# Moving the operands of the main products to other places within 512 bytes, in a windowed attention with a rational feed-forward layer

## The chip, the cores and the metric

The kernel runs on one core of one Trainium2 chip. The metric is the device time of one execution in microseconds; three runs of the kernel before gave 959.98 (median), 959.06 and 960.10 us. A profile of one further execution is read here as "the profile"; the engines in it are PE (TensorE, matrix products), PEld (the loads of stationary operands for them), DVE (VectorE), ACT (ScalarE), POOL (GpSimd) and SP (the queue that issues the transfers).

## What is computed

The reference is a causal attention with a window of 64 positions (8 batches, 8 heads, 576 positions, 64 channels), whose output becomes 4608 tokens of 512 channels, followed by a two-layer feed-forward part with a rational function between the layers:

```python
scores = where(mask, q @ k.T / sqrt(64), -1e9)      # 0 <= i - j < 64
x = (softmax(scores) @ v).transpose(0, 2, 1, 3).reshape(4608, 512)
h = x @ w_in                                         # 512 -> 2048
P = a[0] + a[1]*h + a[2]*h**2 + a[3]*h**3
Q = 1 + abs(b[0])*abs(h) + abs(b[1])*h**2
out = (P / (Q + 1e-6)) @ w_out                       # 2048 -> 512
```

## The kernel before

The tokens are taken in 12 chunks of 384 (`CH`), the 2048 inner channels in 16 blocks of 128. One pair of a chunk and a block is a **step**; there are 192. A step has three parts.

*First layer* (`ffn1`, lines 597 to 607). PE multiplies a 128 x 128 block of `w_in` with the chunk's `x`, 384 tokens wide, for each of the four groups of 128 input channels. To reach fp32 accuracy every operand is kept as two parts, a high one and a low one (`xh`, `xl`, `wi_h`, `wi_l`), and three products are added: `wi_h` with `xl`, `wi_h` with `xh`, `wi_l` with `xh`. That is 4 x 3 = 12 products for a step, each with the weight block as the **stationary** operand (loaded into the array ahead of the product, a PEld row) and 384 columns of `x` as the **moving** operand (streamed through the array, a PE row). All are written to a PSUM tile `h`.

*Gate* (`gate`, lines 609 to 628). ACT and DVE work out the rational function from `h` and leave the result as two parts `gh` and `gl`. Except for four steps at either end this is done for two steps at once, on tiles with two halves of 384 columns.

*Second layer* (`ffn2`, lines 638 to 668). For each of three groups of 128 tokens, PE multiplies 128 columns of `gl` or `gh` (stationary now) with a block of `w_out` (`wo_h`, `wo_l`: moving, 512 columns): 3 x 3 = 9 products for a step, added up over the 16 blocks in three PSUM tiles `o0` to `o2`.

So each core has 192 x 12 = 2304 products of 384 columns and 192 x 9 = 1728 products of 512 columns. While one product streams, the stationary operand of the next one is being loaded: both are read from the same on-chip memory (SBUF), at two addresses in the same partition.

The attention units (12 chunks x 4 pairs of heads) are strewn between the steps: `ps_s<-qk` (scores), the exponentials on ACT, `ps_s<-ident,sm` (transposes on PE) and `ps_x<-sm,vt` (values). They leave the next chunk's `xh` and `xl` in one of two slots (`x_slot`, line 456). The weights are in two halves as well: blocks 0 to 7 in the tiles `wi_h0`, `wi_l0`, `wo_h0`, `wo_l0` of the pool `const`, blocks 8 to 15 in tiles of the pool `late`. All operations are recorded first, by a planner (lines 55 to 277) that gives each a cost and a start, and are issued in the order of those starts; so nearly every row of the profile has line 277.

**Where things lie.** A pool hands out its tiles one behind the other in every partition, each rounded up to 32 bytes, and the three pools `const`, `late` and `ring` follow each other. `shift` (line 377) makes a tile that nothing uses, to move what comes behind it. Adding up the declarations gives each operand's **place**, its address modulo 512. Blocks of `w_in` (512 bytes), of `w_out` (2048), the `x` tiles (1536), the halves of a gate tile (1536) and a gate tile (3072) are all whole multiples of 512 bytes, so that in the kernel before every operand of a kind has one place:

- `const` opens at byte 1152; ident, ident_b, mask, ab_sb, b_sb and warm take 512 + 256 + 1536 + 32 + 32 + 256; the weights begin at 3776, place 192.
- Four weight tiles of 16384, two `top` tiles of 2048 and the shift of 80 words (320 bytes) later, `x` begins at 73728, place 0.
- Sixteen `x` tiles and the shift of 48 words later `late` begins at 98496, place 192 again.
- `ring`, from 164032, has qk (3360), two vt (3072 each), three w_st (4128 each), two sm (3072 each), six small ones (32 each), six tmp (3072 each) and the shift of 32 words; the gate tiles begin at 210816, place 384.

The **distance** of a product is here the place of its stationary operand less that of its moving operand, modulo 512. Before, it is 192 - 0 = 192 in the first layer and 384 - 192 = 192 in the second, six units of 32 bytes in both.

Of the kernel before, what the change touches and what calls it, by code (L numbers as in the profile page):

```python
# [10 lines left out]
F32R = mybir.dt.float32r  # L11
# [10 lines left out]
CH = 384  # L22
# [4 lines left out]
PAIRS = 2, 2  # L27
# [9 lines left out]
JOIN = 4  # L37
LOADS = "q0 q1 w0 v0 q2 v1 q3 w1 v2 v3 w2 w3 w4 w5 w6 w7 w8"
WLEAD = 4
NEG = -8.0e9  # L40
QADD = 1.0 + 1e-6


class Late:


    def __init__(self, key, start, size, get):
        self.key, self.start, self.size, self.get = key, start, size, get
# [239 lines left out]
class Slots:  # L288


    def __init__(self, pool, n, shape, dtype, name):
        self.tiles = [pool.tile([shape[0], 2, *shape[1:]], dtype, name=f"{name}_{k}") for k in range(n)]
        self.n = 0

    def __call__(self, size):
# [16 lines left out]
def swa_rational_ffn(ctx: ExitStack, tc: tile.TileContext, qk, v, w_in, w_out, out):  # L312
    nc = tc.nc
    P = 128
    HP = qk.shape[0]
# [8 lines left out]
    const = ctx.enter_context(tc.tile_pool(name="const", bufs=1))  # L324
    late = ctx.enter_context(tc.tile_pool(name="late", bufs=1))
    ring = ctx.enter_context(tc.tile_pool(name="ring", bufs=1))
# [16 lines left out]
    def make_mask():  # L343
# [3 lines left out]
        def block(j, h, empty):  # L347
            r = mask[half[h], j, :]
            nc.gpsimd.memset(r, 0.0)

            nc.gpsimd.affine_select(out=r, in_=r, pattern=[[1, P]], compare_op=ALU.is_ge, fill=NEG,
                                    base=-WIN if empty else -1, channel_multiplier=0 if empty else -1)

            nc.gpsimd.affine_select(out=r, in_=r, pattern=[[-1, P]], compare_op=ALU.is_ge, fill=NEG, base=WIN, channel_multiplier=1)

# [21 lines left out]
    def shift(pool, words, name):  # L377
        pool.tile([P, words], F32, name=name)

    H = NF // 2  # L380
    W_SHAPES = dict(wi_h=[P, H, NCC, P], wi_l=[P, H, NCC, P], wo_h=[P, H, DO], wo_l=[P, H, DO])
    w_sb = {(n, 0): const.tile(shape, F32R, name=f"{n}0") for n, shape in W_SHAPES.items()}

    def late_tile(name):
        if (name, 1) not in w_sb:
            w_sb[name, 1] = late.tile(W_SHAPES[name], F32R, name=f"{name}1", tag=f"late_{name}")
        return w_sb[name, 1]

    def weight(name, i, view=lambda x: x):
        if i < H:  # L390
            return view(w_sb[name, 0][:, i])
        return Late(f"late_{name}", (i - H) * 2048, 2048, lambda: view(late_tile(name)[:, i - H]))

    def weight_piece(name, i, cc):
        if i < H:
            return w_sb[name, 0][:, i, cc, :]
        return Late(f"late_{name}", (i - H) * 2048 + cc * 512, 512, lambda: late_tile(name)[:, i - H, cc, :])

# [1 line left out]
    for t in tops:  # L400
        nc.vector.memset(t, 0)

    shift(const, 80, "before_x")
    x_sb = [[[const.tile([P, CH], F32R, name=f"x{part}{s}{hp}") for hp in range(HP)] for part in "hl"] for s in range(2)]
    shift(const, 48, "after_x")
    early = [late.tile([P, H * DO], F32, name=f"early{k}", tag=f"late_{n}") for k, n in enumerate(("wo_l", "wo_h"))]
    QK = 2 * CH + WIN
    QKAB = QK + 6
# [9 lines left out]
    sm_ring = Ring(ring, 2, [P, 2, PR, P], F32, "sm")  # L418
    small = {n: Ring(ring, 2, [P, 2 * PR], F32, n) for n in ("nmx", "sums", "rs")}
    tmp = Slots(ring, TMP, [P, CH], F32, "tmp")  # L420
    shift(ring, 32, "before_g")
    g_ring = [Slots(ring, n, [P, CH], F32R, name) for n, name in zip(PAIRS, ("gh", "gl"))]
    ob_ring = Ring(ring, 2, [P, DO], F32, "ob")

    shares = {t.tensor.name: f"late_{n}" for t, n in zip(early + spare, ("wo_l", "wo_h", "wi_h", "wi_l"))}
# [207 lines left out]
    part = {}  # L633
# [38 lines left out]
    def at(s, *call):  # L672
        todo.setdefault(max(s, 0), []).append(call)

    for i in range(H):
        if i >= WLEAD:
            at(i - WLEAD, load_weight, "in", i)
        at(i, load_weight, "out", i)
    second = [("in", i) for i in range(H, H + WLEAD)]
    for i in range(H, NF):  # L680
        if i + WLEAD < NF:
            second.append(("in", i + WLEAD))
        second.append(("out", i))
    for n, key in enumerate(second):
        at(H - 1 + n, load_weight, *key)
    fetch_order += [("in", i) for i in range(WLEAD)]
    fetch_order += [tuple(call[1:]) for s in range(total) for call in todo.get(s, ()) if call[0] is load_weight]

    s, seen, places = 0, {0}, []
# [21 lines left out]
    for load in LOADS.split():  # L711
        what, k = load[0], int(load[1])
# [71 lines left out]
```

## Time and profile before

| | |
|---|---|
| median of three runs | 959.98 us (959.06 to 960.10) |
| the profiled execution's own time | 959.31 us |
| its span, first to last instruction | 957.5 us |
| PE busy, share of the span | 947.7 us, 99% |
| DVE busy | 853.2 us, 89% |
| ACT busy | 666.2 us, 70% |
| products of 384 columns (`h<-...`) | 3 x 768 |
| products of 512 columns (`o<-...`) | 3 x 576 |

Busy time on PE counts each product from its dispatch to its modelled end, so successive products overlap: a row's mean duration (336 ns for 384 columns) is not what a product costs. What it costs is the distance in time from its start to the next one's start, the **spacing**, which is read from the timeline or from the chain of waits, where runs of products are merged with their count.

### The profile page before, as it was taken

What the parts mean: (1) busy time and instruction counts of PE and PEld (TensorE: products, weight loads), DVE (VectorE), ACT (ScalarE), POOL (GpSimd) and SP (SyncE); (2) the same over time, 40 slices, a digit from 0 to 9 for tenths busy, and PEclk for the clock granted to TensorE, in tenths of its full rate; (3) what the DMA queues carried; (4) which work ended last, traced back from release to release, by engine and by line L of the source; (5) the groups of instructions that cost most, each with busy time, mean ns of one, the idle gap of its engine ahead of it and who ended that gap; (6) DMA issues with size and microseconds to landing.
All of it is one profiled execution on the core that took longest, in us unless ns stands there. A gap on an engine that the chain in (4) does not pass through costs nothing.

```text
span 957.5 us, 17342 instructions
## 1 busy us (share of the span) xinstructions
PE 947.7 (99%) x6923; PEld 837.9 (88%) x6923; DVE 853.2 (89%) x1287; ACT 666.2 (70%) x1553; POOL 4.4 (0%) x20
## 2 busy tenths in 40 slices
PE   8999999999999999999999999999999999999998
PEld 6888888898888888888888888888888888888997
DVE  6999998899988899889988998899889988997887
ACT  7988777676676677667667667667666766665654
POOL 1000000000000000000000000000000000000000
PEclk9999999999999999999999999999999999999999
DMA  9454342131101102113112112110210311300000
GB/s 352 135 187 150 104 158 94 58 123 59 47 35 68 53 23 98 35 35 103 35 35 79 60 35 69 42 63 24 80 39 32 102 36 36 102 1 1 34 1 33
DMA packets 24560, 68.36 MB, mean 71 GB/s; under 512 B 2720, under 2 KB 2720, under 8 KB 24480
## 3 DMA queue, kind: packets, MB, share of 16 engines
q1 hardware_dynamic: 24480, 67.27, 20.5%
q8 instruction: 54, 0.88, 0.4%
q14 instruction: 26, 0.21, 0.1%
HBM read 57.03 MB, written 10.22 MB: 70 GB/s over the span
## 4 chain that ended last, share of the span: by engine, by line
PE 84%; DVE 9%; ACT 3%; DMA 2%; issue 1%; POOL 0%; SPq 0%; POOLq 0%; ACTq 0%; DVEq 0%
PE o L277 38%; PE h L277 36%; PE ps_s L277 6%; DVE tmp L277 4%; PE ps_x L277 4%; DVE gh L277 1%; DVE w_st L277 1%; ACT sm L277 1%; DVE gl L277 1%; DMA qk<-qk 1%; DVE wo_l L277 1%; ACT tmp L277 1%; DMA w_st<-w_out 1%; DVE nmx L277 1%; DVE wi_l L277 0%
## 5 line engine op out<-in xcount | busy, mean ns | idle before, releaser
L277 PE MATMUL h<-xl,wi_h 128*128 128x384 f32 x768 | 259.1, 337 | 0.1
L277 PE MATMUL h<-xh,wi_h 128*128 128x384 f32 x768 | 258.1, 336 | 0.0
L277 PE MATMUL h<-xh,wi_l 128*128 128x384 f32 x768 | 257.9, 336 | 0.0
L277 ACT ACTIVATE tmp<-h 128x384 f32<-128x384 f32 x192 | 95.1, 496 | 218.9 <-PE h L277 217.5
L277 PE MATMUL o<-wo_h,gl 128*128 128x512 f32 x576 | 236.1, 410 | 0.8 <-DVE gl L277 0.8
L277 PE MATMUL o<-wo_l,gh 128*128 128x512 f32 x576 | 228.0, 396 | 0.0
L277 PE MATMUL o<-wo_h,gh 128*128 128x512 f32 x576 | 227.7, 395 | 0.0
L277 ACT ACTIVATE tmp<-h,ab_sb 128x384 f32<-128x384 f32 x384 | 221.0, 629 | 0.0
L277 ACT ACTIVATE tmp<-tmp 128x768 f32<-128x768 f32 (+1 forms) x200 | 164.8, 824 | 16.0 <-DVE tmp L277 12.9
L277 PEld LDWEIGHTS h<-xl,wi_h 128*128 128x128 f32 x768 | 144.3, 188 | 8.4 <-DVE tmp L277 0.6
L277 PEld LDWEIGHTS h<-xh,wi_h 128*128 128x128 f32 x768 | 144.3, 188 | 6.8
L277 PEld LDWEIGHTS h<-xh,wi_l 128*128 128x128 f32 x768 | 144.4, 188 | 0.0
L277 DVE SCALAR_TENSOR_TENSOR gh<-tmp,ab_sb,tmp 128x768 fp32r<-128x768 f32 (+1 forms) x100 | 98.5, 985 | 47.8 <-ACT tmp L277 47.5
L277 PEld LDWEIGHTS o<-wo_h,gh 128*128 128x128 f32 x576 | 108.7, 189 | 25.1
L277 PEld LDWEIGHTS o<-wo_h,gl 128*128 128x128 f32 x576 | 108.5, 188 | 24.3 <-issue 6.5
L277 PEld LDWEIGHTS o<-wo_l,gh 128*128 128x128 f32 x576 | 108.7, 189 | 15.9
L277 DVE SCALAR_TENSOR_TENSOR tmp<-tmp,ab_sb,h 128x384 f32<-128x384 f32 x192 | 117.3, 611 | 2.9
L277 DVE SCALAR_TENSOR_TENSOR tmp<-tmp,b_sb,tmp 128x768 f32<-128x768 f32 (+1 forms) x96 | 96.0, 1000 | 25.8 <-ACT tmp L277 25.8
L277 DVE TENSOR_TENSOR tmp<-tmp,h 128x384 f32<-128x384 f32 x192 | 105.2, 549 | 4.4 <-ACT tmp L277 4.4
L277 DVE SCALAR_TENSOR_TENSOR tmp<-tmp,ab_sb,tmp 128x768 f32<-128x768 f32 (+1 forms) x96 | 95.9, 999 | 1.7
L277 DVE SCALAR_TENSOR_TENSOR tmp<-tmp,gh 128x768 f32<-128x768 f32 (+1 forms) x100 | 92.4, 924 | 1.4
L277 ACT ACTIVATE sm<-sm,nmx 128x128 f32<-128x128 f32 x216 | 83.6, 390 | 12.9 <-DVE nmx L277 12.9
(97 smaller groups left out, 817.2 us busy)
## 6 DMA issues: line engine op xcount, KB each, us to landing
qk<-qk SPq DMA_DIRECT2D x42, 419.0 KB, 3.2
vt<-v SPq DMA_DIRECT2D x44, 384.0 KB, 4.0
out<-ob SPq DMA_DIRECT2D x33, 256.0 KB, 2.1
w_st<-w_out SPq DMA_DIRECT2D x15, 512.0 KB, 4.3
w_st<-w_in SPq DMA_DIRECT2D x11, 512.0 KB, 3.3
early<-qk SPq DMA_DIRECT2D x6, 419.0 KB, 8.5
early<-v SPq DMA_DIRECT2D x4, 384.0 KB, 8.8
early_wi_l<-w_in SPq DMA_DIRECT2D x3, 512.0 KB, 10.0
```

The source lines that it names most:

```text
L277: call(*[value(x) for x in args], **{k: value(x) for k, x in kw.items()})
```

## The change

Only places are changed. No operation is added, removed or put in another order.

- A shift of 8 words (32 bytes) ahead of the weights moves their first half from place 192 to 224.
- The shift ahead of `x` is 72 words in place of 80, so `x` stays at 73728, place 0. Behind the eight tiles of each slot there are 16 words (64 bytes): slot 0 stays at place 0, slot 1 comes to place 64.
- The shift ahead of `late` is 88 words (352 bytes): `late`, with the second half of the weights, begins at 98784, place 480.
- The halves of a gate tile are 64 bytes further apart (`G_APART`), a tile takes 3200 bytes, and 64 words are put behind the two tiles of each part. With a shift of 56 words ahead, `gh` begins at 211200, place 256, and `gl` at 217856, place 256. The four halves of each part lie at the places 256, 320, 384 and 448.
- What lies in `ring` moves along: qk from place 192 to 480, vt from 480 to 256, sm from 64 to 352, tmp from 256 to 32.

The first layer's distances are 224 - 0, 224 - 64, 480 - 0 and 480 - 64: 7, 5, 15 and 13 units of 32 bytes. The second layer's are the four gate places less 224 or 480: 1, 3, 5, 7, 9, 11, 13 and 15 units. Together that makes twelve cases, all odd: four with 576 products each and eight with 216 each.

```diff
+X_APART = 16
+G_APART = 16
...
-    def __init__(self, pool, n, shape, dtype, name):
-        self.tiles = [pool.tile([shape[0], 2, *shape[1:]], dtype, name=f"{name}_{k}") for k in range(n)]
+    def __init__(self, pool, n, shape, dtype, name, apart=0):
+        self.tiles = [pool.tile([shape[0], 2, shape[1] + apart], dtype, name=f"{name}_{k}")[:, :, 0:shape[1]] for k in range(n)]
...
+    shift(const, 8, "before_w")
...
-    shift(const, 80, "before_x")
-    x_sb = [[[const.tile([P, CH], F32R, name=f"x{part}{s}{hp}") for hp in range(HP)] for part in "hl"] for s in range(2)]
-    shift(const, 48, "after_x")
+    shift(const, 72, "before_x")
+    x_sb = []
+    for s in range(2):
+        x_sb.append([[const.tile([P, CH], F32R, name=f"x{part}{s}{hp}") for hp in range(HP)] for part in "hl"])
+        shift(const, X_APART, f"after_x{s}")
+    shift(const, 56 + 64 - 2 * X_APART, "before_late")
...
-    shift(ring, 32, "before_g")
-    g_ring = [Slots(ring, n, [P, CH], F32R, name) for n, name in zip(PAIRS, ("gh", "gl"))]
+    shift(ring, 56, "before_g")
+    g_ring = []
+    for n, name in zip(PAIRS, ("gh", "gl")):
+        g_ring.append(Slots(ring, n, [P, CH], F32R, name, G_APART))
+        shift(ring, 64, f"after_{name}")
```

## The prediction

> **What bounds the kernel now.** First the page's shares and its chain of waits, then the chain in order of time between 860 and 950 us, where no attention work is left.
>
> ```profile
> PE 947.7 (99%) x6923; PEld 837.9 (88%) x6923; DVE 853.2 (89%) x1287; ACT 666.2 (70%) x1553; POOL 4.4 (0%) x20
> PEclk9999999999999999999999999999999999999999
> PE 84%; DVE 9%; ACT 3%; DMA 2%; issue 1%; POOL 0%; SPq 0%; POOLq 0%; ACTq 0%; DVEq 0%
> 876.02 4.16 PE h L277 x24
> 880.18 4.20 PE o L277 x18
> 884.38 4.16 PE h L277 x24
> ```
>
> PE is never idle and its granted clock is full all the time, so the chain runs through PE. The last three rows give the price of one product: 24 first-layer products take 4.16 us, 173.3 ns each; 18 of the second layer 4.20 us, 233.3 ns each. The waits and the groups say who waits for whom, and how many products there are:
>
> ```profile
> ACT tmp L277 <- PE h L277: 217.5, 149, 3.4
> PE o L277 <- DVE gl L277: 0.8, 2, 0.6
> ...
> L277 PE MATMUL h<-xl,wi_h 128*128 128x384 f32 x768 | 259.1, 337 | 0.1
> L277 PE MATMUL h<-xh,wi_h 128*128 128x384 f32 x768 | 258.1, 336 | 0.0
> L277 PE MATMUL h<-xh,wi_l 128*128 128x384 f32 x768 | 257.9, 336 | 0.0
> L277 PE MATMUL o<-wo_h,gl 128*128 128x512 f32 x576 | 236.1, 410 | 0.8 <-DVE gl L277 0.8
> L277 PE MATMUL o<-wo_l,gh 128*128 128x512 f32 x576 | 228.0, 396 | 0.0
> L277 PE MATMUL o<-wo_h,gh 128*128 128x512 f32 x576 | 227.7, 395 | 0.0
> ```
>
> ACT waits for PE for 217.5 us; PE waits for the gate's result twice, 0.8 us in all. So 3 x 768 x 173.3 ns = 399 us and 3 x 576 x 233.3 ns = 403 us, 802 of the 957.5 us, are spacing of products, and a nanosecond on each of the 4032 is 4.0 us of time. The change can only act through that spacing, or by slowing an engine that feeds PE.
>
> **Is there anything in the spacing that places could change?** The group of bf16 products has the same 384 columns, and two of them stand merged at 33.72 us:
>
> ```profile
> L277 PE MATMUL ps_s<-mask,ident_b 128*128 128x384 bf16 x20 | 5.0, 330 | 0.9 <-ACT sm L277 0.7
> 33.72 0.49 PE L277 MATMUL ps_s<-mask,ident_b 128*128 128x384 bf16 x2
> ```
>
> The pair lasts 0.49 us, one of them 0.33, so the second starts 0.16 us after the first. A product of the first layer pays 173.3 ns for as many columns, 13 ns more. The same excess at 512 columns is 233.3 - 0.16 x 512/384 = 20 ns. In all 2304 x 13 + 1728 x 20 = 65 us. It may belong to the 4-byte data itself or to the meeting of two readers, for the next stationary operand is fetched during the product:
>
> ```profile
> 501.73 0.19 PEld L277 LDWEIGHTS h<-xh,wi_l 128*128 128x128 f32 x1
> ...
> 501.73 0.33 PE L277 MATMUL h<-xh,wi_h 128*128 128x384 f32 x1
> 501.90 0.33 PE L277 MATMUL h<-xh,wi_l 128*128 128x384 f32 x1
> 502.07 0.33 PE L277 MATMUL h<-xl,wi_h 128*128 128x384 f32 x1
> 502.24 0.34 PE L277 MATMUL h<-xh,wi_h 128*128 128x384 f32 x1
> ```
>
> The load and the product start together. And here three products take 0.51 us, 170 ns each, in place of 173.3. The second layer has such a stretch as well:
>
> ```profile
> 505.73 0.39 PE L277 MATMUL o<-wo_l,gh 128*128 128x512 f32 x1
> ...
> 507.56 0.34 PE L277 MATMUL h<-xl,wi_h 128*128 128x384 f32 x1
> ...
> 509.65 0.40 PE L277 MATMUL o<-wo_h,gl 128*128 128x512 f32 x1
> ...
> 511.74 0.34 PE L277 MATMUL h<-xl,wi_h 128*128 128x384 f32 x1
> ```
>
> From 505.73 to 507.56 are eight products, 228.8 ns each; from 509.65 to 511.74 nine, 232.2 each, the last one at a turn to the other layer. Shapes and distance are equal, and only the stretch before (attention products in the first case) differs. So the spacing depends on how the two streams stand to each other in time, which is what one expects of readers that get into each other's way, and a difference of 4.5 ns (233.3 - 228.8) or 3.3 ns (173.3 - 170) is within reach of it. That is my ground for taking places seriously.
>
> **The parts of the change.**
>
> *Places of the two operands.* The trace has one distance, six units of 32 bytes, for nearly all products, and no odd one. Bounds for an odd one from the nearest rows: on the side of gain the faster stretches, 3.3 and 4.5 ns a product, and at the far end the whole excess, 13 and 20 ns. On the side of loss I take a wait of one 64-byte line of the moving stream. That is 16 columns, and 128 columns cost 233.3 - 173.3 = 60 ns, so 7.5 ns, an estimate. Nothing says that all twelve cases fall alike. I take half of them at one such wait (2016 products x 7.5 ns = 15.1 us), a quarter unchanged, and a quarter at the faster spacing (576 x 3.3 + 432 x 4.5 ns = 3.8 us). [...] Sum: +11.3 us.
>
> *Gate halves 64 bytes further apart.* DVE's pair operations on `gh` and `gl` now skip 64 bytes between two runs of 384. The trace has one operation on one stretch of 768 and on two runs of 384 in separate banks:
>
> ```profile
> L277 DVE TENSOR_REDUCE nmx<-sm 128x6 f32<-128x768 f32 x36 | 34.2, 951 | 0.0
> L277 DVE TENSOR_REDUCE nmx<-ps_s 128x6 f32<-128x768 f32 x10 | 9.6, 955 | 0.8 <-PE ps_s L277 0.8
> L277 DVE TENSOR_TENSOR gl<-tmp,tmp 128x768 fp32r<-128x768 f32 x92 | 87.9, 955 | 1.1
> ```
>
> 4 ns at most; three such operations for each of the 92 pairs make 1.1 us on DVE, beside PE. If that cover went, 1.1 us would be the cost. I take nothing.
>
> *Other tiles moved along in `ring`* (qk, vt, sm, tmp). The first chunk's units have their q, k and v in other tiles, part of them at places that are no multiples of 64 (a unit there is 6424 bytes), and their rows read:
>
> ```profile
> L277 PE MATMUL ps_s<-qk 64*64 64x128 f32 x1008 | 37.2, 278 | 0.4 <-DMA qk<-qk 0.4
> L277 PE MATMUL ps_s<-early 64*64 64x128 f32 x96 | 3.5, 278 | 0.6 <-DMA early<-qk 0.6
> L277 PE MATMUL ps_x<-sm,vt 128*64 128x64 f32 x1056 | 40.4, 226 | 0.0
> L277 PE MATMUL ps_x<-sm,early 128*64 128x64 f32 x48 | 1.9, 226 | 0.0
> ```
>
> 278 and 226 ns in both: nothing. For ACT and DVE on `tmp` no row shows an odd place. One per cent either way on DVE would be 8.5 us of its 853.2, behind a PE that waits for it 0.8 us; I take nothing, and if all that reached PE it would be 8.5 us.
>
> *Waits, queues, transfers.* None is added or moved: dependences, costs and sizes as the planner sees them are the same, so the order is.
>
> Sum: 959.3 (the profiled execution's own time, 0.7 below the median) + 11.3 = 970.6 us. About 0.2%, 2 us, is what a measurement of this kernel can tell from no change.
>
> **The rivals.**
>
> *Places do not matter (959.3 us).* For it: the turns between the layers have other distances. During the last second-layer product of a step the first layer's weights are loaded, 192 - 192 = 0 units; during the last first-layer product a gate tile, 384 - 0 = 12 units.
>
> ```profile
> 501.32 0.39 PE L277 MATMUL o<-wo_h,gh 128*128 128x512 f32 x1
> ...
> 509.47 0.34 PE L277 MATMUL h<-xh,wi_l 128*128 128x384 f32 x1
> ...
> 509.88 0.40 PE L277 MATMUL o<-wo_l,gh 128*128 128x512 f32 x1
> ```
>
> From 501.32 to 501.73 and from 509.47 to 509.88 one product of each layer passes, 0.41 us both times, where steady spacings give 0.407. So distances 0 and 12 cost what 6 costs, within 0.01 us. All three are whole lines of 64 bytes, and the change is the first to leave these: against it stands also that two stretches at one distance differ by 4.5 ns. This rival is also the Trainium skill's view: "TensorE: Matmul & The Clock Gate", section "What happens when you issue a matmul", says that PE reads its streaming operand and its weight loads through two independent SBUF ports, and that the load takes no read bandwidth from the running product. By that rule the sum is zero; the faster stretches at equal shapes speak against it, the turns for it.
>
> *Half a line apart is better (943.9 us).* If the steady spacings hold a wait that comes from both readers standing at the same point of a 64-byte line, an offset of half a line removes it, and all products run at the faster rows: 2304 x 3.3 + 1728 x 4.5 = 15.4 us. It decides as soon as odd distances agree among themselves, so that no mixture is left. At 943.9 us DVE's 853.2 would be 90%, still not the bound. The far end, the whole 65 us, would give 894 us, with DVE at 95%; no stretch of the trace comes near.
>
> *Every odd distance costs one line (989.5 us).* The same mechanism with the other sign: an operand half a line off touches nine lines in each load (first layer) or one more in each stream (second layer), and the extra one is waited for: 4032 x 7.5 = 30.2 us. It is the slow end of my forecast rather than a case of its own.
>
> **How the numbers follow.** The forecast's case, slower by a mixture or by all twelve, 0.48; no difference 0.22; half a line is better 0.30. These are also the chances of slower, same and faster. The range goes from the faster rival, 944, to all twelve at one wait, 990; beyond lie a gain nearer the whole excess and a loss of more than a line. The likeliest case alone goes from 961.3 to 990.
>
> **What the profile after would show.** In the chain, runs of `PE h` and `PE o` between 860 and 950 us: right, if 24 and 18 products no longer take 4.16 and 4.20 us and the steps differ in a rhythm of four (gate places), by weight half and by slot of `x`; then the twelve cases can be read one by one. If all steps are equal among themselves at another spacing, it is the offset of half a line, in either direction, and the mixture is wrong. If the runs stay at 4.16 and 4.20 us, places do not matter. DVE's pair rows should stay within 4 ns of 955, and PE's waits for `gl` near 0.8 us; if those grow, DVE is the cause and not the spacing.

## The result, and the profile after

The changed kernel took 965.83 us (median of four runs, 965.05 to 966.18) against 959.89 us (959.06 to 960.10): a ratio of 1.006, with a 95% interval of 1.0048 to 1.0073. It is 5.9 us slower. The profiled execution took 965.05 us, its span is 963.3 us.

First the page, with the chain's shares, and then the waits. A line of the code now has number 279 instead of 277.

```profile
span 963.3 us, 17342 instructions
PE 954.6 (99%) x6923; PEld 843.0 (88%) x6923; DVE 853.4 (89%) x1287; ACT 665.6 (69%) x1553; POOL 4.3 (0%) x20
PEclk9999999999999999999999999999999999999999
PE 92%; DVE 3%; ACT 3%; DMA 1%; issue 1%; POOL 0%; POOLq 0%; ACTq 0%
```

```profile
ACT tmp L279 <- PE h L279: 226.6, 153, 3.5
PE o L279 <- DVE gl L279: 0.9, 2, 0.7
```

The number of instructions is the same, the clock is full, DVE and ACT are as busy as they were (853.4 for 853.2, 665.6 for 666.2 us). Only PE is busier, 954.6 us for 947.7, and ACT waits longer for it, 226.6 us for 217.5. So nothing that feeds PE is in the way; PE itself takes longer over the same work. Where, the chain in order of time shows, in the stretch without attention (start in us, duration, what):

```profile
885.30 4.20 PE o L279 x18
889.50 4.23 PE h L279 x24
893.74 4.21 PE o L279 x18
897.95 4.24 PE h L279 x24
902.19 4.19 PE o L279 x18
```

24 first-layer products take 4.23 to 4.24 us, for 4.16 before: 176.5 ns each in place of 173.3. 18 of the second layer take 4.19 to 4.21 us, for 4.20.

That holds for the whole span. Adding up the time from the start of each product to the start of the next one, where both are of the same layer, gives 370.3 us before and 375.9 after for the first layer (2128 intervals, 174.0 and 176.6 ns), and 359.7 and 360.7 us for the second (1512 intervals). All other intervals together changed by -0.9 us. So the first layer alone makes 5.6 us, as much as the span grew by (5.7), and the rest cancels. The order of the instructions on PE is the same, product by product, in both traces.

The twelve cases can be read apart, since each step's weights, slot and gate half are known. Each case must be held against the same steps of the kernel before, where all have distance 6. This table is worked out from the starts in the two traces. It has the mean spacing of products with a neighbour of the same layer on both sides, in ns:

| layer | distance, units of 32 bytes | the same steps before, at 6 | after |
|---|---|---|---|
| first | 5, 7, 13, 15 | 173.2, 174.0, 173.2, 173.2 | 176.5, 175.5, 176.3, 175.7 |
| second | 1, 3, 5, 7 | 233.2, 232.9, 230.0, 233.3 | 232.4, 233.6, 233.1, 233.5 |
| second | 9, 11, 13, 15 | 233.4, 232.9, 230.3, 232.8 | 232.2, 233.9, 232.9, 233.5 |

All four cases of the first layer lost, 1.5 to 3.3 ns. Cases whose distances differ by 8 units, 256 bytes, agree within 0.2 ns there.

In the second layer a gate place is also a position among four successive steps, and the attention units come back every four steps as well. So its columns differ already before, where the distance is one: the third step of every four, whose second layer stands right behind an attention unit's score products, has 230.0 and 230.3 ns. Against the same steps the second layer lost 3.1 and 2.6 ns in these (distances 5 and 13), and the other six lie between 1.2 ns below and 1.0 above. Another kernel with all distances at 6 ("Everything half a line off", below) differs from these groups by up to 1.3 ns, so no price can be read from those six.

The rows beside PE, which the prediction had put at nothing:

```profile
L279 DVE TENSOR_TENSOR gl<-tmp,tmp 128x768 fp32r<-128x768 f32 x92 | 87.8, 954 | 1.1
L279 PE MATMUL ps_s<-qk 64*64 64x128 f32 x1008 | 37.2, 278 | 0.0
L279 PE MATMUL ps_x<-sm,vt 128*64 128x64 f32 x1056 | 40.4, 226 | 0.0
```

954 ns for 955, 278 for 278, 226 for 226: neither the gap in the gate tiles nor the tiles moved along cost anything.

### The profile page after: what moved, and what is told of

Same layout as the page of the kernel before. It is cut to its first block, busy times and chain, and to the rows that moved or that the text cites. A ratio compares the mean times of both kernels' runs of the same rounds, so it can differ in the third digit from the quotient of the medians.

```text
span 963.3 us, 17342 instructions
## 1 busy us (share of the span) xinstructions
PE 954.6 (99%) x6923; PEld 843.0 (88%) x6923; DVE 853.4 (89%) x1287; ACT 665.6 (69%) x1553; POOL 4.3 (0%) x20
## 4 chain that ended last, share of the span: by engine, by line
PE 92%; DVE 3%; ACT 3%; DMA 1%; issue 1%; POOL 0%; POOLq 0%; ACTq 0%
PE o L279 42%; PE h L279 40%; PE ps_s L279 6%; PE ps_x L279 4%; DVE tmp L279 1%; ACT tmp L279 1%; ACT sm L279 1%; DMA w_st<-w_out 1%; DVE nmx L279 0%; ACT top L279 0%; DVE gh L279 0%; DVE gl L279 0%; DVE wi_l L279 0%; DVE sm L279 0%; DVE w_st L279 0%
## 5 line engine op out<-in xcount | busy, mean ns | idle before, releaser
L279 ACT ACTIVATE tmp<-h 128x384 f32<-128x384 f32 x192 | 95.1, 495 | 226.9 <-PE h L279 226.6
```

Of the source, the lines that this page charges most:

```text
L279: call(*[value(x) for x in args], **{k: value(x) for k, x in kw.items()})
```

## The experiments

Four explanations stood at the start. A: the first layer's stationary operand is off a line of 64 bytes. B: the distance is an odd number of 32-byte units. C: the many places keep PE from one rhythm. And the rival that places do not matter, which would need another cause for the 5.9 us. All kernels below differ from the kernel before, or from the changed one where it is said, only in the lines shown; every ratio is to the kernel before. A "line of 64 bytes" is here only a stretch that begins at a multiple of 64; no run shows that the chip reads in such stretches.

### Weights alone half a line off

```diff
+    shift(const, 8, "before_w")
...
-    shift(const, 80, "before_x")
+    shift(const, 72, "before_x")
...
-    shift(const, 48, "after_x")
+    shift(const, 56, "after_x")
...
+    shift(ring, 120, "before_qk")
```

> Weights alone 32 bytes off (place 224 in both halves), x at 0, gate tiles at 384, the tiles of ring at their old places: one odd distance in each layer, 7 in the first and 5 in the second. Theory A (the first layer's stationary operand off lines of 64 bytes costs its products 2 to 3 ns, whatever the distance): 24 first-layer products take about 4.23 us instead of 4.16, the time is about 966 us. Theory B (an odd distance costs it): the same, 966. Theory C (it is the variety of places, which keeps the streams from settling into one rhythm): steady at 4.16, 960 us.

Measured: 964.65 us, ratio 1.0056 (1.0044 to 1.0069). Without the two slots, without the four gate places, with one odd distance in each layer, nearly the whole loss is there. C falls. But the loss lies elsewhere in part: added up as above, the intervals of the first layer grew by 3.2 us and those of the second by 2.8, for 5.6 and 1.0 in the changed kernel. The chain in order of time, early and late:

```profile
183.00 2.12 PE h L277 x12
191.85 4.24 PE h L277 x24
...
209.82 4.17 PE h L277 x24
...
248.50 2.08 PE h L277 x12
...
889.41 4.17 PE h L277 x24
893.58 4.19 PE o L277 x18
```

At 183 us a step's 12 products take 2.12 us, 176.7 ns each, and at 192 us 24 take 4.24, as in the changed kernel. Others take 4.17 or 2.08, nearly as before, and in the undisturbed stretch all take 4.17 from 881 us on. So an odd distance is not always slow: at this one, 7, slow and fast steps alternate where attention units stand between them, and all are fast where none do.

### The other operands half a line off

The same odd distances from the other side: x and gate tiles moved, the weights left.

```diff
-    shift(const, 80, "before_x")
+    shift(const, 88, "before_x")
...
-    shift(const, 48, "after_x")
+    shift(const, 40, "after_x")
...
-    shift(ring, 32, "before_g")
+    shift(ring, 40, "before_g")
```

> x and the gate tiles 32 bytes off instead of the weights (x at 32, gate at 416, weights at 192): distances 5 and 7, odd; now the moving operand of the first layer and the stationary one of the second are off lines of 64. Theory A, carried over to the second layer: the first layer stays at 4.16 us for 24, the second's 18 products take some 2 to 3 ns more each, 4.24 us instead of 4.20, time about 964 us; A for the first layer alone: 960. Theory B: the first layer slow as in the changed kernel, 966 us. Theory C: 960 us.

Measured: 966.00 us, ratio 1.0062 (1.0048 to 1.0076).

```profile
890.60 4.23 PE h L277 x24
894.83 4.19 PE o L277 x18
```

The first layer is slow at 4.23 us, although its stationary operand is on a line of 64 again. Its intervals grew by 6.7 us, those of the second layer by 0.1. A falls, in both forms: the second layer, whose stationary operand is off a line now, stays at 4.19.

### Everything half a line off

```diff
+    shift(const, 8, "before_w")
...
+    shift(ring, 120, "before_qk")
...
-    shift(ring, 32, "before_g")
+    shift(ring, 40, "before_g")
```

> Weights, x and gate tiles all 32 bytes off lines of 64 (224, 32, 416): both distances are 6 again, even, as before. Theory A: the first layer is slow, since its stationary operand is off a line: 966 us or more. Theory B: both distances are even, so all is as before, 960 us. Theory C: 960 us.

Measured: 959.53 us, ratio 0.9998 (0.9989 to 1.0006).

```profile
182.95 2.08 PE h L277 x12
191.71 4.16 PE h L277 x24
...
892.55 4.16 PE h L277 x24
896.71 4.20 PE o L277 x18
```

All three kinds of operand lie 32 bytes off lines of 64, and every spacing is as before. So for this move of 32 bytes it is the distance between two operands that counts, not the place of any one of them. This also answers the rival: places matter through distances.

### The changed kernel with even distances

```diff
-    shift(const, 8, "before_w")
...
-    shift(const, 72, "before_x")
+    shift(const, 80, "before_x")
...
-    shift(const, 56 + 64 - 2 * X_APART, "before_late")
+    shift(const, 48 + 64 - 2 * X_APART, "before_late")
...
-    shift(ring, 56, "before_g")
+    shift(ring, 64, "before_g")
```

(against the changed kernel)

> The changed kernel with its weights back on lines of 64 (places 192 and 448): gate parts at four places, weights at two, x at two, and twelve even distances (4, 6, 12, 14 in the first layer, 0 to 14 in the second). Theories A and B: 960 us, both layers at their old spacing if even distances are alike. Theory C (variety): 966 us. If single distances differ, the steps differ by gate place, weight half or x slot, and a distance better than 6 would show here.

Measured: 960.46 us, ratio 1.0007 (0.9998 to 1.0015). The variety is the same as in the changed kernel, the loss is gone. But even distances are not alike, and the time is a balance: the first layer's intervals grew by 2.4 us, those of the second shrank by 1.8. Worked out as in the table above, in ns:

| layer | distance | the same steps before, at 6 | spacing |
|---|---|---|---|
| first | 4, 12 | 173.2, 173.2 | 175.7, 175.7 |
| first | 6, 14 | 174.0, 173.2 | 173.3, 173.3 |
| second | 2, 10 | 233.2, 233.4 | 233.4, 233.3 |
| second | 4, 12 | 232.9, 232.9 | 232.5, 232.6 |
| second | 6, 14 | 230.0, 230.3 | 230.0, 230.3 |
| second | 0, 8 | 232.8, 233.3 | 228.8, 228.8 |

So B in its plain form falls as well: 4 and 12 are even, and cost the first layer 2.5 ns, about what the odd ones cost. The first layer's price repeats after 256 bytes. In the second layer distances 0 and 8 are better than 6, by 4.0 and 4.5 ns; the others differ from the same steps before by 0.4 ns at most.

### Distance 0 in the second layer

```diff
-    shift(ring, 32, "before_g")
+    shift(ring, 112, "before_g")
```

> The kernel before with its gate tiles at place 192 in place of 384, like the weights: distance 0 in the second layer, 6 in the first. In the run with twelve even distances the second layer's steps at distances 0 and 8 had 228.3 ns a product against 233.3 at the steady distance 6. Theory D (each distance modulo 256 bytes has a rhythm of its own, and 0 is better than 6): 18 products take 4.11 us or less instead of 4.20, first layer 4.16 as before; 1728 x 5 ns = 8.6 us, about 951 to 952 us. Theory E (those steps were fast because of what came before them in that mixture): 4.20 us, 960 us.

Measured: 954.57 us, ratio 0.9948 (0.9936 to 0.9961): the fastest kernel of this study, ahead of the kernel before by 5 us and of the changed one by 11.

```profile
888.81 4.16 PE h L277 x24
892.97 4.09 PE o L277 x18
897.06 4.16 PE h L277 x24
```

Theory D holds, with less than it forecast. In the undisturbed stretch 18 products take 4.09 us in place of 4.20, 227.2 ns each. Over the span the second layer's intervals shrink by 4.9 us, not by 8.6. The forecast took 228.3 against 233.3 ns on all 1728 products, but the span's means are 228.9 and 232.3, over 1512 intervals. The third step of every four, at 230.0 and 230.3 ns before, gained next to nothing (230.2 and 229.9).

### Two other distances in the first layer

Each in addition to the edit above; x at place 192, then at 128.

```diff
-    shift(const, 80, "before_x")
+    shift(const, 128, "before_x")
...
-    shift(const, 48, "after_x")
```

> As the run with distance 0 in the second layer, and x at place 192 too: distance 0 in both layers. If what is good for 512 columns is good for 384, the first layer gains as well: 2304 x 3 to 5 ns = 7 to 12 us more, about 940 to 945 us. If a multiple of four units is bad for the first layer (distances 4 and 12 cost it 2.3 ns a product in the mixture of even distances): about 957 us.

```diff
-    shift(const, 80, "before_x")
+    shift(const, 112, "before_x")
...
-    shift(const, 48, "after_x")
+    shift(const, 16, "after_x")
```

> As the run with distance 0 in the second layer, and x at place 128: distance 2 in the first layer, the last even one not yet seen there. If parity is all: first layer as before, 4.16 us for 24, about 952 us. If each distance has its own spacing: another value, between 4.08 and 4.24 us for 24, 948 to 956 us.

Measured: 961.75 us, ratio 1.0022 (1.0013 to 1.0030), for distance 0; 959.95 us, ratio 1.0000 (0.9991 to 1.0009), for distance 2. Both lie above all that was expected of them. The chain of the first and then of the second:

```profile
887.49 4.18 PE h L277 x24
891.68 4.12 PE o L277 x18
```

```profile
885.66 4.24 PE h L277 x24
889.90 4.08 PE o L277 x18
```

Distance 0, good for 512 columns, costs the first layer 0.02 us for 24 even where it is undisturbed (175.7 ns over the span, worked out as in the tables), and distance 2, though even, 0.08. The second layer has distance 0 in these two kernels and in the one before them, and takes 4.12, 4.08 and 4.09 us, although only x was moved: it depends on the first layer's operands as well.

### 16 bytes

All x tiles become slices of one tile, which begins 16 bytes ahead of them; nothing else moves.

```diff
-    x_sb = [[[const.tile([P, CH], F32R, name=f"x{part}{s}{hp}") for hp in range(HP)] for part in "hl"] for s in range(2)]
-    shift(const, 48, "after_x")
+    x_all = const.tile([P, 4 + 4 * HP * CH + 4], F32R, name="x_all")
+    x_at = lambda n: x_all[:, 4 + n * CH:4 + (n + 1) * CH]
+    x_sb = [[[x_at((2 * s + part) * HP + hp) for hp in range(HP)] for part in range(2)] for s in range(2)]
+    shift(const, 40, "after_x")
```

> The kernel before with x 16 bytes off (all sixteen x tiles in one tile, place 16): distance 176 bytes, 5.5 units, in the first layer; nothing else moves. If the two streams meet in lines of 64 bytes, and only the share of a line counts, the first layer lies between distance 6 (4.16 us for 24) and 5 (4.23): about 963 us. If a grain of 32 bytes counts and 16 stay within it: 960 us. If the grain is 16 bytes: any value, with its own rhythm.

Measured: 958.61 us, ratio 0.9987 (0.9978 to 0.9996).

```profile
884.37 4.20 PE h L277 x24
888.58 4.14 PE o L277 x18
```

The first layer is half way between 4.16 and 4.23, as the first reading expected, but the time isn't. What none expected: the second layer, none of whose operands moved, takes 4.14 us in place of 4.20, and the kernel comes out 1 us faster. Over the span the first layer's intervals grew by 1.8 us and those of the second shrank by 3.4. So a layer's spacing depends on the other layer's operands too.

### Does the stream meet the next load, or its own operand?

In both kernels xl and wi_l alone are 32 bytes off; the second also changes the order of each three products.

```diff
-    w_sb = {(n, 0): const.tile(shape, F32R, name=f"{n}0") for n, shape in W_SHAPES.items()}
+    w_sb = {(n, 0): const.tile(W_SHAPES[n], F32R, name=f"{n}0") for n in ("wi_h", "wo_h", "wo_l")}
+    shift(const, 8, "before_wi_l")
+    w_sb["wi_l", 0] = const.tile(W_SHAPES["wi_l"], F32R, name="wi_l0")
...
-    shift(const, 80, "before_x")
-    x_sb = [[[const.tile([P, CH], F32R, name=f"x{part}{s}{hp}") for hp in range(HP)] for part in "hl"] for s in range(2)]
-    shift(const, 48, "after_x")
+    shift(const, 72, "before_x")
+    x_h = [[const.tile([P, CH], F32R, name=f"xh{s}{hp}") for hp in range(HP)] for s in range(2)]
+    shift(const, 8, "before_xl")
+    x_l = [[const.tile([P, CH], F32R, name=f"xl{s}{hp}") for hp in range(HP)] for s in range(2)]
+    x_sb = [[x_h[s], x_l[s]] for s in range(2)]
+    shift(const, 40, "after_x")
...
-    spare = [late.tile([P, H * NCC * P], F32, name=f"early_{n}", tag=f"late_{n}") for n in ("wi_h", "wi_l")]
+    spare = []
+    for n in ("wi_h", "wi_l"):
+        if n == "wi_l":
+            shift(late, 8, "before_late_wi_l")
+        spare.append(late.tile([P, H * NCC * P], F32, name=f"early_{n}", tag=f"late_{n}"))
...
+    shift(ring, 120, "before_qk")
```

> The kernel before with its two low parts of the first layer alone 32 bytes off: xl at place 32, wi_l at 224; xh at 0, wi_h at 192, the second layer unchanged. Two of three first-layer products have an odd distance, whether it is taken to the product's own stationary operand (wi_h less xl is 5, wi_l less xh is 7, wi_h less xh is 6) or to the one loaded during it, the next one's (xl with wi_h 5, xh with wi_l 7, xh with wi_h 6). By both readings the first layer is slow: 24 products in 4.19 to 4.24 us, 963 to 967 us. If two thirds do not suffice, 960 us.

```diff
-                    for w, x in (("wi_h", 1), ("wi_h", 0), ("wi_l", 0)):
+                    for w, x in (("wi_h", 1), ("wi_l", 0), ("wi_h", 0)):
```

> The same places, but each group of three first-layer products is taken in the order wi_h xl, wi_l xh, wi_h xh; the sum is the same but for the order of adding. Then a product's own distances are 5, 7 and 6 as before, but the operand loaded during it has the distances 6, 6 and 6 (xl with wi_l, xh with wi_h, xh with wi_h). If the meeting is between a product's stream and the load of the next stationary operand: back at 4.16 us for 24, 960 us. If it is the product's own stationary operand, or the places by themselves: slow as with the other order, 963 to 967 us.

Measured: 963.63 us, ratio 1.0042 (1.0029 to 1.0055), in the old order; 958.57 us, ratio 0.9986 (0.9978 to 0.9995), in the new one. The chain of the one and of the other:

```profile
890.13 4.24 PE h L277 x24
894.37 4.12 PE o L277 x18
```

```profile
893.07 4.20 PE h L277 x24
897.27 4.12 PE o L277 x18
```

With every tile where it was, another order takes 5.1 us away. A product's own pairs are the same in both orders, and two of three are odd; only the pairs of a stream with the *next* load became even. But most of that time does not come from the first layer. In the two profiled executions, whose spans differ by 5.7 us, its intervals differ by 2.3 us, those of the second layer, whose operands and order are the same, by 1.8, and all others by 1.6. The first layer had lost 5.6 us by the two low parts and keeps 3.3 of them; it came down to 4.20 us for 24, not to 4.16. The reading "next load" expected all of it back, the reading "own operand" none. So this leans to the meeting with the next load and does not show it. Besides, the new order was not run with all tiles at their old places, so that a part may belong to the order itself.

### Gate at 192 and x 16 bytes off, to either side

Both have x in one tile, as in the 16-byte kernel, and the second-layer edit; the second has x at place 496 in addition.

```diff
-    shift(ring, 32, "before_g")
+    shift(ring, 112, "before_g")
```

```diff
-    shift(const, 80, "before_x")
+    shift(const, 72, "before_x")
...
-    shift(const, 40, "after_x")
+    shift(const, 48, "after_x")
```

> Gate tiles at place 192 (distance 0 in the second layer) and x 16 bytes off (5.5 units in the first). If the two layers' gains add up: second layer 4.09 us for 18 or the 4.08 that it kept behind another first layer, first layer 4.20 as with x 16 bytes off alone: 8.28 to 8.29 us for two steps against 8.25 with distance 6, about 957 us. If the layers set each other's rhythm, the first layer takes another value: 950 to 960 us.

> Gate tiles at place 192 and x 16 bytes off to the other side (place 496, 208 bytes, 6.5 units in the first layer). If 16 bytes to either side are alike, as the run with x at place 16: 957 us. If what counts is how far the load is ahead of the stream, a first layer below 4.16 us for 24 is possible: 948 to 952 us.

Measured: 957.13 us, ratio 0.9972 (0.9961 to 0.9983), and 959.54 us, ratio 0.9999 (0.9990 to 1.0007).

```profile
891.33 4.16 PE h L277 x24
895.49 4.12 PE o L277 x18
```

```profile
892.87 4.20 PE h L277 x24
897.06 4.11 PE o L277 x18
```

With x at place 16 the first layer is back at 4.16 us, where the same distance had 4.20 beside the old gate places. The sum of the two rows, 8.28 us, is what the first reading expected, but neither of its terms is. With x at place 496 the first layer takes 4.20 us, so neither reading of that run holds: the two sides are not alike, and the first layer is not below 4.16. For neither layer is the distance alone enough to tell its spacing.

## Why the prediction was right in sign and too large

**What bounds the kernel** held: the loss is PE's own, and nothing else moved. The price of a nanosecond held too: 2.6 ns on the first layer's intervals made 5.6 us.

**That places could change the spacing** was argued from two stretches at equal shapes and distance with different spacings. The runs bear it out: moving the operands against each other by 32 bytes costs 0.6%, moving them together nothing (1.0062 and 0.9998). The ground itself was weaker than it looked. The fast stretch at 505.73 us is the third step of four, which stands behind attention products, and these steps have 230.0 and 230.3 ns over the whole kernel before, at the same distance. They show that the spacing can vary, not that places make it vary. The Trainium skill ("TensorE: Matmul & The Clock Gate", section "What happens when you issue a matmul") has it that loading the next stationary operand takes no read bandwidth from the running product. The runs here disagree: distances worth 0.5% either way (1.0056 and 0.9948) are not what independent reads would give. Which two reads meet, and what makes them meet, no run shows.

**The size** is the term that failed, twice over. The prediction took half of the twelve cases at 7.5 ns, one line of the moving stream, and a quarter at a gain of 3.3 to 4.5 ns; the sum was +11.3 us, where 5.9 were measured. Against the same steps before, no case lost more than 3.3 ns and none gained more than 1.2. The first layer lost in all four of its cases, 5.6 us together; the second lost about 3 ns in two of its eight, and 1.0 us in all. So both the price and the split were off. No run shows the line of 64 bytes from which the price was worked out, and a move of 16 bytes already took the first layer from 4.16 to 4.20 us. That the sign came right is in part luck: it rests on taking more cases for losing than for gaining, for which no row spoke; the faster stretches, its only rows, spoke for a gain.

The far bound, 13 and 20 ns of excess over bf16 products, rested on one pair. By their starts, six of the ten pairs in that group stand 172 to 177 ns apart, as far as the first layer's products, and only three at the 162 ns that was read as 0.16 us. So that group gives no ground for an excess of 65 us.

**The gate halves and the tiles moved along** cost nothing, as taken.

**The rivals.** "Places do not matter" rested on the turns between the layers, where distances 0 and 12 cost 0.41 us for two products like distance 6. That reading could not tell: its rows are given to 0.01 us, 10 ns, and the differences are smaller. In the run with even distances the first layer pays 175.7 ns at distance 12, not 173.2, and in the run with distance 0 the second pays 228.9, not 232.3. "Half a line is better" is refuted by the two kernels with one half-line offset, 1.0056 and 1.0062. Of what the profile after was to show, the first layer's spacing changed, and its steps differ by slot of x (175.5 and 175.7 ns in one, 176.5 and 176.3 in the other), but not by weight half. Of the rhythm of four little showed: in the undisturbed stretch the second layer's pieces go between 4.19 and 4.21 us.

## What to carry to other kernels

Where products run back to back, the spacing of their starts is the number to watch, and two operands' addresses, taken against each other, can be worth half a per cent in either direction; moving everything together by 32 bytes was worth nothing. Try the few distances in one kernel, each on its own share of the steps, and read them apart in the trace, but against the same steps of the kernel before: groups of steps can differ without any change of distance. Then build the best one, since a share among others does not promise the same for the whole. A good distance for one shape may be a poor one for another.

## What the runs showed of the hardware that was not expected

In the first layer the price repeats after 256 bytes: distances 8 units apart agree within 0.2 ns in all four pairs of the two tables, odd and even, where the other slot's steps of the same kernel differ by 0.7 to 2.5 ns. In the second layer the eight pairs agree within 0.3 ns, but a pair takes the same steps of every four, and these agree within 0.5 ns before as well, at one distance. So there only distances 0 and 8 speak for the period, as both are faster. The best and the worst distance of the first layer lie 3.2 ns apart in the tables (173.3 and 176.5); in the second, distances 0 and 8 lie 4.0 and 4.5 ns below distance 6 in the same steps. And a layer's spacing is not its own affair: with x moved by 16 bytes, the second layer ran at 4.14 us for 18 instead of 4.20, without a change to its own operands.
